# Four more channel units hand their four products to TensorE without an addition on VectorE, in a kernel ordered by hand-kept tables

## The chip, the cores and the metric

One core of one Trainium2 chip runs the kernel. The metric is the device time of one execution in microseconds, as a median over executions. A second number is the span of the profiled execution, from its first to its last recorded instruction.

## The reference

Two layers work on the same 2048 rows of 512 channels, and a gate mixes them. Cut to what is computed:

```python
g = sigmoid((x * gate_w).sum(-1, keepdims=True))
# a: a state-space convolution, 512 channels, 128 states each
dt = exp(log_dt)[:, None]; A = A_re + 1j*A_im; B = B_re + 1j*B_im; C = C_re + 1j*C_im
K = einsum("dn,dnl,dn->dl", C, exp((dt*A)[:,:,None] * arange(L)), dt*B).real   # kernel, L = 2048
y = irfft(rfft(pad(x.T)) * rfft(pad(K)))[:, :L].T                              # y in bf16
a = y + x * Dskip
# b: linear attention, 32 heads of 16, feature maps of two softmaxes
q, k, v = split(x @ wqkv)
phi(t) = concat(softmax(t @ w_phi), softmax(-(t @ w_phi)))
num = phi(q) @ (phi(k).T @ v);  den = phi(q) @ phi(k).sum(rows) + 1e-6
b = (num / den) @ wo
out = g * a + (1 - g) * b          # (1, 2048, 512), bf16
```

## The kernel before

**Front.** Parameters, `u` and the weights are loaded; twiddle tables (`TB`, `TI`, `TJ`) are made with sines on ScalarE; `wps` folds the feature map into the key and query weights (`WW`, `Wqp`); `xps` transposes `u` into `xT`. Polar forms of the state parameters become the tables `Ctab` and `Dtab`. The spectrum of `u` is made in two stages of matmuls, `psA` read out as `XAu` and `psB` read out as `xst`, and written to memory (`XUd`). The keys go in eight blocks of 256 rows: `pk` on TensorE, two exponentials `Ek` on ScalarE, a sum per head and sign `Zk` on VectorE, its inverse on ScalarE, `vp` read out as `vb`, the product `vr` on VectorE and `kn` (tile `kvp`) on TensorE. In some blocks TensorE first adds groups of four (`zk`, L718), which leaves VectorE a shorter reduction (L734 in place of two of L731).

**Convolution kernel.** The 512 channels are cut into 16 units of 32 (unit U holds channels 32U to 32U+31). For a unit the power of a state at position l is split in a coarse and a fine factor, both complex. ScalarE makes the fine factor's sines and cosines (`cs`) and its magnitude (`E`), VectorE extends `E` (`El`, L1049) and multiplies both into `R` (`Rh` L1119, `Rl` L1123). The coarse factor `A` is made from `Ctab` and `Dtab` by two products, L1102 and L1107. They are the real and the imaginary part of a sum, which a third instruction, L1112 (`A3`), forms in a unit whose digit in `FOURS` is 0; TensorE then contracts two parts of `A` with two of `R` in 64 matmuls. Where the digit is 1 there is no addition and TensorE takes all four products, 128 matmuls that add up in PSUM (L170, tile `kps`). `A` has one buffer, `R` two.

**Transforms.** `kps` is read out as `KD`, transformed (`psA` read out as `XA`, `psB` as `XK`), multiplied with the stored spectrum (`XUX`, product `t`, L1233, or L1236 for the last two units), transformed back (`psz`, read out as `Zr`; then through memory, `Zd` and `ZT`, or by a transpose on VectorE for the last 128 channels) and finished in `psy`, where the attention's output is added for the first three blocks of 128 channels; VectorE multiplies by the gate (L1370, L1373). The units of one 128-channel block share a transform; the last block's units 14 and 15 go singly.

**What sets the order.** Every step is a node of one plan (`Plan.add`, L102); nothing is scheduled by a compiler. `run` (L148) gives each engine its instructions in the order of the table `ORDER`, two letters a node. `SIDES` has one digit for each step that may run on either of two engines, mostly the read-outs out of PSUM: ScalarE or VectorE (`evict`, L562; helpers L144 on ScalarE, L146 on VectorE). `RINGS` says from which PSUM pool such a step takes its buffer. `WARM` gives the number of dummy matmuls that TensorE issues into a new PSUM tile ahead of its work (L1563); a digit counts only where the node takes a new tile. `ZPS` marks the key blocks with the pre-sum on TensorE. An engine works strictly in its own order, so an instruction that waits holds all behind it.

Buffers (L1440): `A`, `KD`, `XA`, `ax` one each; `R`, `E`, `XK`, `Zr` two; `XUX` three; `cs` four.

Of the kernel before, what the change touches and what calls it, by code (L numbers as in the profile page):

```python
# [70 lines left out]
class Plan:  # L71

    DIGITS = "0123456789abcdefghijklmnopqrstuvwxyzABCDEFGHIJKLMNOPQRSTUVWXYZ-_"
    ORDER = ("0B0C0D0H0I0J2P000K0L0M112R2t2v0S0U0_100V120W0P0y0z0A2y2u0N0T14150O0Q0Y0X0Z18172Q2S2w2x0405060s0t0u0d0e0f0708090g0h0i0102030j"
             "0k0l0a0b0c0m0n0o0p0q0r0v0w0x130R2T2V2U2W2X2Z2Y2J2K192-0-1a1c1u2H1w1l162I1F2_311x1m1y1n1d1G1H3330322z2A341v2B2F2D1b2C352E1e1A"
             "1C2G1z361D2N2L2O37392M1o1p1q0E0F0G1r1s1t1B1E1W3a1J384A4H4J4I4K4W4Y4X4Z4O4L3b3d4S4M4P3e4N4T4Q4U1N3c513f554R4V3h4-3g563i4_5052"
             "5357595a5b5c5d3j5g1O3k543l585k5l5o5p5h3m5e5f1K5i4B5q4C5m5r5s3P5t3n5v5z3p5j5n3o5w5A1I1Q5u5D5E5F5G5H3u1L3q5x5B3w3x5K5O5y5C5S5L"
             "4D3v5P1R3r3s3t3y3z3A5T5I3Q3R5J5M5Q5U5Z1S5V1X1T1U1P3B3D3E615N5W625X5Y3C5R5-4E635_653I673K1M66683J3L3S6064696k6m3T3V6l6n6o6c6a"
             "6p3W3U6b6q6d3X3Z3Y6r3_3-1V1Z1Y406e1-1_25216s206t6v41433M3N3O3F3G3H1f1g1h426g45444647492627484a4b4c4d4e4g284f4h6h2b6i292a2d2c"
             "224i4j4k4l4n4o2e2m2f232g242h6w2i2j2n4m2o6f6j2q2p2r2k4s4t4p4q4r1i1j1k2l2s4u4v4w4x4y4z6E6G8j6x8x8y6u8i8n8k8m8o8l6y8p8q4F8u6z4G"  # L80
             "8z6D8v8w8A8B6F6H6I8D8E8R6K7b8C8F8J8K8G8H8I6J6L6M8S7c6N7d7f7haf6O8X8T7e7g6P6Q8Yag7i8L7K8-7M6R6S6T6U9c9d9e6V6W6X6Z6-6_8M8_7j8N"
             "7O8P7L8O7k8Q7N8U8V94907l957m7n8W8Z7Pao7Qap7oa5a9aa919293ah6Y707p7q7r6A6B6C9f9g9h9i9j9k7s7t7u7w7x7y9697a6a87173abadalamaq74ai"
             "aj72akauav98759a99a79bacae7RanaC777SaD9o7T789p76aras7vaE7U7VataI7Wawax9waL7A7C9x9q9y7XaM7D9r9z9s9AaJc6c77zaFaG9EbY7E7G7FaN7Y"
             "7Z7-7_80818384858r8s8t9B9C9D9t9u9v9l9m9nb0b1b2c09Fc17BaRaHc882869GaSb-c39M9NayaA87azaBaKb_7H88898b7Ic4aOaPaQ9Occcd8abZ8c7J8d"
# [6 lines left out]
    SIDES = ("01110001001011111100111001000001010101110000001110000000000011101000101111111100010100010000000000000000000000000000"  # L91
             "0000000000000000000000000010000000000000000001100001001")
# [4 lines left out]
    FOURS = ("0111110101011000")  # L97
    ZPS = ("00000101")
# [1532 lines left out]
```

## Time and profile before

| | |
|---|---|
| median of 3 runs | 252.7 us (251.59 to 253.8) |
| profiled execution, its own time | 252.06 us |
| its span | 250.3 us |
| VectorE (DVE) busy | 234.2 us, 94% |
| ScalarE (ACT) busy | 221.2 us, 88% |
| TensorE (PE) busy | 206.6 us, 83% |
| mean granted TensorE clock | 0.957 |
| transfers | 34.86 MB, 139 GB/s |

"L178" is line 178 of the kernel, and a row names the tile written, an arrow, and the tiles read. In the rows of groups stand the count, the busy time, the mean of one in ns, and the idle time just before with its releaser; in the rows of the timeline the start, the length, and in brackets the wait before. In the rows of waits stand who waited for whom, the total, how often and the longest. L144 and L146 are helpers, so read-outs are told apart by their tiles.

### The profile page before, as it was taken

The page shows a single profiled execution, that of the slowest core. Times are in us where ns is not written, and L with a number is a line of the kernel's source. Part 1 is how long each engine was busy: PE and PEld are TensorE (multiplying, and loading weights), DVE is VectorE, ACT ScalarE, POOL GpSimd, SP SyncE. Part 2 cuts the span into 40 slices and gives each one's busy share as a digit, 9 for nine tenths or more (in the row PEclk, how much of TensorE's full clock was granted, in tenths as well). Part 3 has the DMA queues.
Part 4 walks back from the last instruction along what each step waited for, and adds up shares of the span by engine and source line. Part 5 has one row for each costly group of instructions (what it writes and reads, how often), then busy time and mean ns, then how long its engine had stood idle before and what let it go on. Part 6 is the DMA issues. An engine that isn't in the chain of part 4 may idle for free. (4 is left out here: it accounts for less than half of the span.)

```text
span 250.3 us, 9879 instructions
## 1 busy us (share of the span) xinstructions
PE 206.6 (83%) x4393; PEld 141.3 (56%) x4415; DVE 234.2 (94%) x318; ACT 221.2 (88%) x305; POOL 8.7 (3%) x21
## 2 busy tenths in 40 slices
PE   0675999999984685999988887999989789889960
PEld 0675656555754432365656645775678467777530
DVE  7999998899999999999999999999999999998880
ACT  3998998999999999999999999999999997892830
POOL 5700000000000000000000000000000000000000
PEclk9999999999997596899999999999999999999996
DMA  7997000080551755003787049723595989872934
GB/s 187 220 218 182 18 3 4 3 243 14 145 151 59 198 150 146 3 3 115 182 245 185 5 122 204 245 86 66 157 245 133 237 230 319 197 226 50 220 75 84
DMA packets 52842, 34.86 MB, mean 139 GB/s; under 512 B 30528, under 2 KB 48320, under 8 KB 52800
## 3 DMA queue, kind: packets, MB, share of 16 engines
q1 hardware_dynamic: 51744, 33.98, 53.4%
q8 instruction: 34, 0.56, 0.9%
q10 hardware_dynamic: 1056, 0.26, 0.5%
q14 instruction: 8, 0.07, 0.1%
HBM read 21.38 MB, written 12.58 MB: 136 GB/s over the span
## 5 line engine op out<-in xcount | busy, mean ns | idle before, releaser
L178 PE MATMUL kps<-R,A 128*32 128x64 bf16 x1600 | 29.1, 229 | 2.5 <-ACT XK L144 0.8
L178 PEld LDWEIGHTS <-A 128*32 128x32 bf16 x1600 | 27.2, 160 | 6.5 <-issue 3.0
L68 ACT ACTIVATE cs<-args 128x1024 bf16<-128x1024 f32 x32 | 30.6, 1050 | 0.0
L1102 DVE TENSOR_TENSOR A<-Ctab,Dtab 128x2048 bf16<-128x2048 bf16 x16 | 19.5, 1218 | 0.6 <-PE kps L178 0.6
L1123 DVE TENSOR_TENSOR R<-E,cs 128x2048 bf16<-128x2048 bf16 x16 | 19.5, 1218 | 0.0
L1107 DVE TENSOR_TENSOR A<-Ctab,Dtab 128x2048 bf16<-128x2048 bf16 x16 | 19.5, 1218 | 0.0
L1119 DVE TENSOR_TENSOR R<-E,cs 128x2048 bf16<-128x2048 bf16 x16 | 19.5, 1217 | 0.0
L144 ACT CAST XA<-psA 128x1024 bf16<-128x1024 f32 (+1 forms) x17 | 16.1, 986 | 2.5 <-PE psA L185 2.4
L144 ACT CAST Zr<-psz 128x1024 bf16<-128x1024 f32 (+1 forms) x16 | 15.8, 1025 | 2.0 <-DMA Zd<-Zr 1.6
L68 ACT ACTIVATE Ek<-pk 128x512 bf16<-128x512 f32 x32 | 16.6, 611 | 1.0 <-PE pk L704 1.0
L68 ACT ACTIVATE E<-args 128x1024 bf16<-128x1024 f32 x16 | 16.8, 1052 | 0.4 <-issue 0.2
L68 ACT ACTIVATE Eq<-pq 128x512 bf16<-128x512 f32 (+1 forms) x28 | 16.8, 688 | 0.3 <-PE pq L838 0.3
L1233 DVE TENSOR_TENSOR t<-XUX,XK 128x2048 bf16<-128x2048 bf16 x14 | 16.9, 1219 | 0.1
L144 ACT CAST XK<-psB 128x1024 bf16<-128x1024 f32 (+1 forms) x17 | 16.1, 981 | 0.6 <-DVE t L1233 0.6
L838 PE MATMUL pq<-xT,Wqp 128*128 128x512 bf16 x64 | 16.5, 395 | 0.1
L752 PE MATMUL vp<-WW,xT 128*128 128x512 bf16 x62 | 15.7, 380 | 0.1
L704 PE MATMUL pk<-WW,xT 128*128 128x512 bf16 x57 | 14.8, 380 | 0.5 <-issue 0.2
L611 PE MATMUL psB<-XAu,TB 64*128 64x128 bf16 x256 | 11.0, 241 | 3.8 <-ACT xst L144 2.6
L731 DVE TENSOR_REDUCE Zk<-Ek 128x64 f32<-128x1024 bf16 x12 | 14.0, 1210 | 0.0
L65 ACT ACT_TABLE_LOAD x10 | 12.8, 1283 | 0.9 <-PEq L1615 0.7
L611 PEld LDWEIGHTS <-TB 64*128 64x128 bf16 x256 | 9.0, 106 | 8.0 <-issue 7.9
L761 DVE TENSOR_TENSOR vr<-vb,vr 128x1024 bf16<-128x1024 bf16 x16 | 10.5, 683 | 1.7 <-ACT vr L68 1.5
(213 smaller groups left out, 506.4 us busy)
## 6 DMA issues: line engine op xcount, KB each, us to landing
XUX<-XUd SPq DMA_DIRECT2D x32, 256.0 KB, 4.9
XUd<-xst SPq DMA_DIRECT2D x8, 512.0 KB, 3.0
ax<-apd SPq DMA_DIRECT2D x16, 256.0 KB, 5.1
Zd<-Zr SPq DMA_DIRECT2D x24, 128.0 KB, 3.5
ZT<-Zd SPq DMA_DIRECT2D x6, 512.0 KB, 6.1
UD<-in_A_u_dram SPq DMA_DIRECT2D x16, 128.0 KB, 4.2
XUd<-xst SPq DMA_DIRECT2D x8, 256.0 KB, 4.0
wqk<-in_B_wqkv_dram SPq DMA_DIRECT2D x1, 1024.0 KB, 5.5
```

Source lines behind the costliest of these rows:

```text
L68: return self.nc.scalar.activation(**kw)
L144: self.nc.scalar.copy(out=o, in_=i)
L178: nc.tensor.matmul(kps[32 * dj:32 * dj + 32, g4, e, :], lhsT=A[:, ka, :, :, d].rearrange("p a b -> p (a b)"), rhs=R[:, kr, d, :], start=(i ...
L611: nc.tensor.matmul(box.ps[:, c2, sl, :], lhsT=fc.TB[rows, b0:b0 + 2].rearrange("p a b -> p (a b)"), rhs=X.t[rows, k, r0 + sl].rearrange("p ...
L704: nc.tensor.matmul(box.ps[:], lhsT=xT[:, st, kt, :], rhs=g.WW[:, kt, :], start=(kt == 0), stop=(kt == 3))
L752: nc.tensor.matmul(box.ps[:], lhsT=xT[:, st, kt, :], rhs=g.WW[:, 4 + kt, :], start=(kt == 0), stop=(kt == 3))
L838: nc.tensor.matmul(box.ps[:, m - m0, :] if late else box.ps[:], lhsT=g.Wqp[:, kt, 128 * m:128 * m + 128], rhs=xT[:, 4 * b:4 * b + 4, kt, : ...
L1102: nc.vector.tensor_tensor(out=c.A[:, 0:2].rearrange("p o a b c -> p (o a) b c"), in0=g.C[U // 8][:, 0:2, :, d0 % 256:d0 % 256 + 32].rearra ...
L1107: nc.vector.tensor_tensor(out=c.A[:, 2:4].rearrange("p o a b c -> p (o a) b c"), in0=g.C[U // 8][:, 1:3, :, d0 % 256:d0 % 256 + 32].rearra ...
L1119: nc.vector.tensor_tensor(out=c.R[:, :, :, 32:64], in0=t.E[:, 1].unsqueeze(1).to_broadcast([128, 2, 32, 32]), in1=t.cs[:], op=ALU.mult)
L1123: nc.vector.tensor_tensor(out=c.R[:, :, :, 0:32], in0=t.E[:, 0].unsqueeze(1).to_broadcast([128, 2, 32, 32]), in1=t.cs[:, ::-1, :, ::-1], o ...
L1233: nc.vector.tensor_tensor(out=box.t, in0=Ls[r0 // ns].X[:], in1=box.XK[:].unsqueeze(1).to_broadcast([128, 2, 1024]), op=ALU.mult)
```

## The change

`FOURS` has four more ones: units 0, 6, 8 and 10 lose the addition L1112 and get 128 matmuls in place of 64. Only units 13, 14 and 15 keep it. `ZPS` loses a one: a single key block (the eighth) keeps the pre-sum on TensorE, and the sixth goes back to two long reductions on VectorE. `ORDER`, `SIDES`, `RINGS` and `WARM` are new tables. The digits of `WARM` add up to 57 before and 76 now; in the built programs stand 45 dummy matmuls before and 61 now.

```diff
-    FOURS = ("0111110101011000")
-    ZPS = ("00000101")
+    FOURS = ("1111111111111000")
+    ZPS = ("00000001")
...
-    WARM = ("00000000000000610000000000002000060000000000000040000010000030000000000500050203000040000041500000000000100020000000"
+    WARM = ("00000000302140230000000500010000000000500005000002000021010153506010000100200200010000000300300200000000000000000000"
...
-    ORDER = ("0B0C0D0H0I0J2P000K0L0M112R2t2v0S0U0_100V120W0P0y0z0A2y2u0N0T14150O0Q0Y0X0Z18172Q2S2w2x0405060s0t0u0d0e0f0708090g0h0i0102030j"
+    ORDER = ("0B0C0D0H0K0L0I0J2P0M0_000S0U0P0N0O0V102t2u110W0405060y0z0A0s0t0u0a0b0c0g0h0i0102030d0e0f0j0k0l0708090m0n0o0p0q0r0v0w0x17120Q"
```

Read-outs change their engine in both directions. VectorE has now nine `XAu` in place of five, five `xT` out of `xps` in place of two, a `KD` of 1024 columns, two `XK` of 1024 and one of 512 and two `xT` of 512, which it had none of; it has four `vb` fewer, and one `xst`, one `WW`, two `wT`, two small `KD` and one small `xT` fewer. ScalarE has the others.

On VectorE, where the keys begin, just ahead of the first reduction of `Ek` to `Zk` (`psA` to `XAu` is the spectrum's first stage). Before:

```order
L377 TENSOR_TENSOR pt_226<-pmag,ppx 128x512
L412 TENSOR_SCALAR pb_228<-pt_227 128x256 x4
L146 CAST XAu<-psA 128x256x4
L731 TENSOR_REDUCE Zk<-Ek 128x64 x2
L146 CAST vb<-vp 128x512 x2
L761 TENSOR_TENSOR vr<-vb,vr 128x2x512 x2
L731 TENSOR_REDUCE Zk<-Ek 128x64 x2
```

The same place on VectorE now:

```order
L377 TENSOR_TENSOR pt_219<-pmag,ppy 128x512
L146 CAST XAu<-psA 128x256x4 x2
L377 TENSOR_TENSOR pt_219<-pmag,ppx 128x512
L731 TENSOR_REDUCE Zk<-Ek 128x64 x2
L146 CAST vb<-vp 128x512
L761 TENSOR_TENSOR vr<-vb,vr 128x2x512 x2
L731 TENSOR_REDUCE Zk<-Ek 128x64 x2
L146 CAST XAu<-psA 128x256x4 x2
```

Four read-outs of `XAu` stand here in place of one, one of `vb` has gone to ScalarE, and the four `pb` steps come later.

On VectorE at unit 6, in the middle of the program (`oT` is read out of the attention's `ops`). Before:

```order
L1102 TENSOR_TENSOR A<-Ctab_75,Dtab 128x2048
L1107 TENSOR_TENSOR A<-Ctab_75,Dtab 128x2048
L146 CAST oT_1977<-ops 128x512
L1049 TENSOR_TENSOR E<-E,Gtab 128x1024
L146 CAST oT_1976<-ops 128x512
L1119 TENSOR_TENSOR R<-E,cs 128x64x32
L1112 TENSOR_TENSOR A<-A 128x2048
```

Unit 6 on VectorE now:

```order
L1102 TENSOR_TENSOR A<-Ctab_75,Dtab 128x2048
L1123 TENSOR_TENSOR R<-E,cs 128x64x32
L909 TENSOR_TENSOR Eq<-Eq,ax 128x2048
L146 CAST oT_2011<-ops 128x512
L146 CAST XK<-psB 128x1024
L1107 TENSOR_TENSOR A<-Ctab_75,Dtab 128x2048
L146 CAST oT_2012<-ops 128x512
L1119 TENSOR_TENSOR R<-E,cs 128x64x32
L146 CAST oT_2011<-ops 128x512
```

The addition L1112 is gone, and a read-out of `XK` with 1024 columns, ScalarE's before, stands between the two products.

On VectorE in the last stage, from the third block's last output product (L1370) on; `t` out of `XUX` and `XK` is the product of the last 128 channels. Before:

```order
L1370 TENSOR_TENSOR xT<-psy,gT 128x4x128
L1233 TENSOR_TENSOR t<-XUX,XK 128x2048 x2
L146 CAST KD<-kps 128x256 x2
L1236 TENSOR_TENSOR t<-XUX,XK 128x2x512
L1373 TENSOR_TENSOR xT<-psy,gT 128x2x4x128
L146 CAST xT<-bps 128x2x128
L1236 TENSOR_TENSOR t<-XUX,XK 128x2x512
```

The last stage on VectorE now:

```order
L1370 TENSOR_TENSOR xT<-psy,gT 128x4x128
L1233 TENSOR_TENSOR t<-XUX,XK 128x2048
L1373 TENSOR_TENSOR xT<-psy,gT 128x2x4x128
L146 CAST XK<-psB 128x1024
L1233 TENSOR_TENSOR t<-XUX,XK 128x2048
L1236 TENSOR_TENSOR t<-XUX,XK 128x2x512 x2
L146 CAST XK<-psB 128x512
L1236 TENSOR_TENSOR t<-XUX,XK 128x2x512 x2
```

The two `t` of 2048 no longer stand together: an output product and a new read-out of `XK` come between them. Two small `KD` and an `xT` have left for ScalarE, and a second `XK` stands ahead of the last two short products.

42 lines of the change are left out of this document (21 added, 21 removed).

## The prediction

> **What bounds the kernel now.** I read the page first, then the busy time by stage, then what VectorE waited for.
>
> ```profile
> span 250.3 us, 9879 instructions
> PE 206.6 (83%) x4393; PEld 141.3 (56%) x4415; DVE 234.2 (94%) x318; ACT 221.2 (88%) x305; POOL 8.7 (3%) x21
> ```
>
> VectorE (DVE) is the fullest engine: 234.2 of 250.3 us. The stages below are cut at VectorE's own landmarks: the first key reduction (29.39), the end of the spectrum's last read-outs `XAu` (72.23), the first `El` (102.50), the third channel block's first products `t` (200.59), its last output product (226.89), the last instruction (243.21). Columns: stretch, length, then the busy time of PE, PEld, DVE, ACT, POOL, then the granted clock, the DMA share and GB/s.
>
> ```profile
> 0.00:29.39 29.39, 17.35 (x174) 14.65 (x176) 27.84 (x66) 24.21 (x33) 8.70 (x21) 1.00 0.84 176
> 29.39:72.23 42.84, 42.14 (x745) 25.81 (x750) 39.71 (x51) 40.59 (x77) 0.00 (x0) 1.00 0.28 82
> 72.23:102.50 30.27, 20.67 (x313) 11.18 (x316) 29.73 (x56) 29.64 (x33) 0.00 (x0) 0.72 0.40 115
> 102.50:200.59 98.09, 88.49 (x2203) 61.89 (x2208) 97.17 (x108) 96.46 (x129) 0.00 (x0) 1.00 0.55 143
> 200.59:226.89 26.30, 23.23 (x603) 18.75 (x599) 24.85 (x25) 21.03 (x23) 0.00 (x0) 1.00 0.83 229
> 226.89:243.21 16.32, 14.77 (x381) 9.03 (x379) 14.85 (x20) 9.27 (x15) 0.00 (x0) 1.00 0.58 131
> 243.21:250.30 7.09, 0.00 (x0) 0.00 (x0) 0.00 (x0) 0.00 (x0) 0.00 (x0) 0.68 0.43 76
> ```
>
> The second stage is TensorE's (42.14 of 42.84); there VectorE idles 3.13 us. From 72 to 200 us VectorE idles 0.54 and 0.92 us, so there a microsecond put on it or taken off it moves the end by one. The last two working stages hold 1.45 and 1.47 us of its idle time. These are its waits:
>
> ```profile
> DVE vr L761 <- ACT vr L68: 1.5, 3, 0.7
> DVE xT L1370 <- PE psy L1360: 1.3, 1, 1.3
> DVE t L1236 <- DMA XUX<-XUd: 1.0, 1, 1.0
> DVE Zk L734 <- PE zk L725: 0.6, 2, 0.4
> DVE A L1102 <- PE kps L178: 0.6, 1, 0.6
> ```
>
> So the question is what the change does to VectorE's own sum, and whether these waits grow or shrink.
>
> **The change part by part.** VectorE's prices:
>
> ```profile
> L1112 DVE TENSOR_TENSOR A<-A 128x2048 bf16<-128x2048 bf16 x7 | 8.5, 1218 | 0.0
> L731 DVE TENSOR_REDUCE Zk<-Ek 128x64 f32<-128x1024 bf16 x12 | 14.0, 1210 | 0.0
> L146 DVE CAST vb<-vp 128x512 bf16<-128x512 f32 x11 | 7.5, 685 | 0.4 <-PE vp L752 0.3
> L146 DVE CAST XAu<-psA 128x1024 bf16<-128x1024 f32 x5 | 5.9, 1217 | 0.3 <-PE psA L586 0.3
> L146 DVE COPY wT<-wtp 128x1024 bf16<-128x1024 bf16 x4 | 2.6, 678 | 0.0
> L734 DVE TENSOR_REDUCE Zk<-zk 128x128 f32<-128x512 f32 x2 | 1.4, 692 | 0.6 <-PE zk L725 0.6
> L146 DVE COPY xT<-xps 128x1024 bf16<-128x1024 bf16 x2 | 1.4, 681 | 0.0
> ```
>
> ```profile
> 114.71 1.22 DVE L1102 TENSOR_TENSOR A<-Ctab,Dtab 128x2048 bf16<-128x2048 bf16 x1
> 115.85 1.22 DVE L1107 TENSOR_TENSOR A<-Ctab,Dtab 128x2048 bf16<-128x2048 bf16 x1
> ```
>
> The two products of the second fence start 1.14 us apart, 0.08 less than one lasts: instructions overlap by that much. So what VectorE pays per instruction is the mean less 0.08: 1.14 for a 1218 ns one, 0.60 for one of 680 to 690 ns.
>
> *First three stages, to 102.5 us.* Gone: unit 0's addition (1.14), four `vb` (2.42), one `xst` (1.14, as `XAu`), one `WW` (1.13, same form as `XAu`), two `wT` (1.20), one `zk` reduction (0.61): 7.6 us. Added: four `XAu` (4.55), three `xT` (1.80), two full key reductions because one block's pre-sum on TensorE is switched off (2.26): 8.6 us. Sum +1.0. (The gate's two 128x16 instructions go from this stage to the next; I leave them out of both.) On ScalarE up to the first `E`:
>
> ```profile
> L144 ACT CAST XAu<-psA 128x1024 bf16<-128x1024 f32 x11 | 10.8, 1023 | 0.2 <-PE psA L586 0.2
> L144 ACT CAST vb<-vp 128x512 bf16<-128x512 f32 x5 | 2.9, 601 | 0.4 <-PE vp L752 0.4
> L144 ACT COPY xT<-xps 128x1024 bf16<-128x1024 bf16 x6 | 6.0, 1013 | 1.0 <-PE xps L499 1.0
> ```
>
> ```profile
> 33.61 1.93 ACT L144 CAST XAu<-psA 128x1024 bf16<-128x1024 f32 x2
> ```
>
> Two in a row last 1.93 us, so the second adds 0.91, and ScalarE's overlap is some 0.12; one costs 0.90, a `vb` 0.48: four `XAu` go (-3.6), three `xT` (-2.7), and come four `vb` (+1.9), an `xst` and a `WW` (+1.8), two `wT` (+1.8), and a pair of `Eq` now ahead of the first `E` (+0.95): +0.15. TensorE loses eight `zk` matmuls, one 1.1 us piece:
>
> ```profile
> 58.41 1.09 PE L725 MATMUL zk<-Ek,ident 128*128 128x256 bf16 x8
> ```
>
> and it is the full engine of the second stage, where VectorE's +1.0 can hide in 3.13 us of idle time. Bounds: +1.0 if nothing hides, -1.5 if half of that idle time goes. I take -0.4, half of TensorE's 1.1 less one dummy, since ScalarE's +0.15 at the next hand-over stops more.
>
> *Fourth stage, to 200.6 us.* Gone: three additions (units 6, 8, 10), -3.42. Added: an `XK` (1.14) and a `KD` (1.14; neither form stands on VectorE before, the nearest is `XAu`, also 1024 columns out of PSUM, and no row is dearer), and two `xT` of 512 columns (1.20, as `vb`): +3.48. An `Eq` product leaves the stage and an `R` enters it. Sum +0.1. **The saving of the change is spent here on read-outs that ScalarE did.** ScalarE gets about 2.8 us lighter, but it was not the last to arrive. I keep the 0.58 wait:
>
> ```profile
> 171.27 1.23 DVE L1102 TENSOR_TENSOR A<-Ctab,Dtab 128x2048 bf16<-128x2048 bf16 x1 [0.58 <-PE kps L178]
> ```
>
> *TensorE's side.* A unit's kernel product costs, with two and with four products:
>
> ```profile
> 105.51 1.21 PE L178 MATMUL kps<-R,A 128*32 128x64 bf16 x64 [0.51 <-DVE R L1123]
> ...
> 110.55 2.25 PE L178 MATMUL kps<-R,A 128*32 128x64 bf16 x128
> ```
>
> So +1.04 for each of four units, 4.2 us, and 16 ns for one more matmul. The built programs hold 45 dummies before and 61 now (the table's 76 counts some that are never issued), 16 more. It hides under VectorE's 98 us, where TensorE has 9.6 us free. [...]
>
> *Fifth stage.* The same work in another order. It is set by the chain from the last `t` through the transfers of `Zr` and `ZT` to `psy`, whose end VectorE awaited for 1.25 us. Order and rings along it are alike; I take 0, from -1.4 (its idle time gone) to +0.5.
>
> *Last stage.*
>
> ```profile
> 226.89 0.69 DVE L1370 TENSOR_TENSOR xT<-psy,gT 128x512 bf16<-128x512 f32 x1 [1.25 <-PE psy L1360]
> 227.50 2.35 DVE L1233 TENSOR_TENSOR t<-XUX,XK 128x2048 bf16<-128x2048 bf16 x2
> ...
> 233.62 0.69 DVE L1236 TENSOR_TENSOR t<-XUX,XK 128x1024 bf16<-128x1024 bf16 x1 [1.05 <-DMA XUX<-XUd]
> ```
>
> ```profile
> 228.74 1.62 SPq L1188 DMA_DIRECT2D XUX<-XUd  x2
> ```
>
> The last `XUX` load goes out when the first `t` frees its buffer (228.6) and is there at 233.62, 5.0 us later. Now an output product, a 1024 `XK` and the other `t` (1.14 each) and one `t32` (0.60) stand between: 4.0 us, so a wait of 1.0 remains and hides the large `XK` as it hid `KD` and `xT` before. The 512 `XK` (0.60) comes after it, uncovered. I take +0.5, from 0 to +0.9 (a later `Zr` for the three transposes that now stand together). Two of the late stores go to ScalarE's queue behind its last read-out, as two others did: nothing.
>
> **Sum:** -0.4 + 0.1 + 0 + 0.5 = +0.2 us. The profiled execution took 252.06 us (span 250.3 and 1.76 around it), so 252.3. That lies just under the median of the runs shown, 252.7, and among them (251.59 to 253.8), so I make no further correction. The terms' bounds, which won't all fall to one side, make 250.8 to 254.0 for this case alone.
>
> **The rivals.**
>
> *The waits go (faster).* The order is new everywhere, so it may pack better. If the front takes its lower bound (-1.5), the 0.58 wait goes against +0.1, and the 1.25 us before the output product goes too while the tail costs +0.5: -1.5 - 0.5 - 1.25 + 0.5 = -2.75, 249.3 us. For it: TensorE, full in the second stage, loses a 1.1 us `zk` there, and half of the 0.6 us that VectorE waited for `zk` goes with it. Against it: the 1.25 us end with transfers, and no shorter path for them shows in the order.
>
> *TensorE is late at kernel products (slower).* `A` has one buffer, so unit u+1's first product waits until unit u's matmuls have read it, and now units 0 to 12 all read it for 2.25 us, where four of them took 1.21. The place: after unit 8's 128 matmuls TensorE has 16 `psB`, 16 `pq` and four `args` before unit 9's.
>
> ```profile
> 171.92 1.89 PE L838 MATMUL pq<-xT,Wqp 128*128 128x512 bf16 x8
> 181.47 1.06 PE L191 MATMUL psB<-XA,TB 128*128 128x128 bf16 x16
> 179.93 0.39 PE L1041 MATMUL args<-selE,statE 64*128 64x512 bf16 x2
> ```
>
> That is 2.25 + 1.06 + 3.7 + 0.7 + 2.25 = 10.0 us from the end of unit 8's second product to the end of unit 9's matmuls. VectorE meanwhile does two `E`, the next `R` and `A` pairs (5.8), another `R` pair and two `t` (4.5): 10.3. Then comes the `KD` read-out, new on VectorE, and it waits for just these matmuls; unit 10's products and all that follows on VectorE are queued behind it. So 0.3 us of lateness decides. If each of units 8 to 12 brings the 0.58 us of the row at 171.27, that is +2.9, and 252.06 + 0.2 + 2.9 = 255.2. Against it: one such wait in all of before.
>
> [...]
>
> *It does less than it says:* VectorE loses four additions and still gains 1.0 + 0.1 in the first four stages and, in the last, the two `XK` (1.74) less two small `KD` and an `xT` that go to ScalarE (about 0.33 each, an estimate from their 128x256 form at a quarter of `XAu`): 1.8 us of work in all. That is in the forecast.
>
> **How the numbers follow.** Likeliest (252.3): 0.58. Waits go (249.3): 0.23. TensorE late (255.2): 0.19. About 1% (2.5 us) is what a measurement here can tell from no change, so against 252.7 faster means below 250.2 and slower above 255.2. Faster: 0.18 of the second case and 0.02 of the first, 0.20. Slower: 0.12 of the third (it may come only in part) and 0.02 of the first, 0.14. The same: 0.66. For 8 in 10 the range runs from 249.3 to 255.4, to about the middle of either rival.
>
> **What would show it.** VectorE's busy sum near 236 us, against 234.2, whatever the span; if it falls, my count is wrong. ScalarE near 217. Unit rows of 128 kernel matmuls at 2.25 us thirteen times. A first `El` near 102.1. The waits on `psy` and `XUX` near 1 us each. Waits of `A` or `KD` on `kps` over 1.5 us in all mean the slower rival; a second stage with under 2 us of VectorE's idle time and no `psy` wait mean the faster one. The prediction is wrong if VectorE's idle time before its last instruction, 9.0 us in before (243.21 less 234.2), moves by more than 2 us.

## The result, and the profile after

Both kernels were timed side by side, 18 executions each. The changed kernel takes 254.39 us (253.34 to 256.46), the kernel before 253.37 us (251.41 to 254.57). The ratio is 1.0066, with a 95% interval of 1.0044 to 1.0087. So it lies within the 1% that was called no change, but it is slower by more than its interval, where the sum had said 0.2 us over the profiled execution. The profiled execution of the changed kernel took 254.0 us, 1.9 more than that of before (252.06). Ratios, here and below, leave out executions that took over 1.5% longer than the fastest of the same kernel: none of these 36, but three of the six of after_phase, for example.

The head of its page, then the stages cut at the same VectorE landmarks (columns as before: stretch, length, busy time of PE, PEld, DVE, ACT, POOL, granted clock, DMA share, GB/s):

```profile
span 252.2 us, 10424 instructions
PE 213.5 (85%) x4679; PEld 144.8 (57%) x4679; DVE 235.7 (93%) x317; ACT 217.9 (86%) x303; POOL 8.2 (3%) x21
```

```profile
0.00:29.79 29.79, 19.25 (x178) 15.73 (x179) 28.34 (x63) 24.77 (x34) 8.21 (x21) 1.00 0.83 173
29.79:71.67 41.88, 40.73 (x739) 25.00 (x738) 40.20 (x52) 40.62 (x76) 0.00 (x0) 1.00 0.33 90
71.67:101.41 29.74, 22.26 (x341) 11.05 (x341) 29.40 (x54) 29.71 (x36) 0.00 (x0) 1.00 0.47 134
101.41:202.35 100.94, 92.70 (x2445) 65.14 (x2446) 97.70 (x110) 92.05 (x121) 0.00 (x0) 0.98 0.48 130
202.35:229.87 27.52, 23.83 (x602) 18.61 (x596) 24.85 (x24) 21.16 (x23) 0.00 (x0) 1.00 0.76 222
229.87:245.67 15.80, 14.77 (x398) 9.31 (x392) 15.15 (x20) 9.63 (x17) 0.00 (x0) 1.00 0.55 129
```

VectorE's sum is 235.7 us, where 236 was forecast, and ScalarE's 217.9, where 217 was. The lengths tell where the 1.9 us of the span came from:

| stage | before | after | change | forecast |
|---|---|---|---|---|
| first three, to the first `El` | 102.50 | 101.41 | -1.09 | -0.4 |
| fourth, to the third block's `t` | 98.09 | 100.94 | +2.85 | +0.1 |
| fifth, to the last output product | 26.30 | 27.52 | +1.22 | 0 |
| last | 16.32 | 15.80 | -0.52 | +0.5 |
| behind VectorE's last instruction | 7.09 | 6.53 | -0.56 | 0 |

In the fourth stage VectorE is busy 0.53 us longer (97.17 before) and idle 2.32 us longer (3.24 against 0.92). In the fifth its work is the same 24.85 us, so all of the 1.22 is waiting. The rows of these waits on VectorE's timeline, the wait in brackets:

```profile
133.80 1.23 DVE L909 TENSOR_TENSOR Eq<-Eq,ax 128x2048 bf16<-128x2048 bf16 x1 [1.38 <-DMA ax<-apd]
177.73 2.36 DVE L1233 TENSOR_TENSOR t<-XUX,XK 128x2048 bf16<-128x2048 bf16 x2 [0.73 <-DMA XUX<-XUd]
218.39 0.69 DVE L1370 TENSOR_TENSOR xT<-psy,gT 128x512 bf16<-128x512 f32 x1 [1.21 <-PE psy L1360]
220.52 0.69 DVE L1049 TENSOR_TENSOR E<-E,Gtab 128x1024 bf16<-128x1024 bf16 x1 [1.43 <-ACT E L68]
```

Only the third has a like in the fourth and fifth stage of before, and that one stood at another place there. What the first two wait for stands on SP's queue (start, length of the issuing, tiles, how many):

```profile
121.89 3.59 SPq L1186 DMA_DIRECT2D XUX<-XUd  x6
126.70 2.81 SPq L902 DMA_DIRECT2D ax<-apd  x4
...
151.51 21.06 SPq L1276 DMA_DIRECT2D Zd<-Zr  x8
172.67 2.45 SPq L1186 DMA_DIRECT2D XUX<-XUd  x4
```

`ax` has one buffer. It is free at 126.67, when the two products of the first batch row end; the loads go out at 126.70, behind 1.5 MB of `XUX`, and VectorE wants the result from 132.42 on; it is there at 133.80. In before the same product started at 137.52. The second place is SP's own order: eight `Zd` stores, of which the last four wait for their `Zr`, hold the four `XUX` loads back until 172.67, and the first `t` needs one 5 us later. In before those loads went out from 154.34 on. The fifth stage's wait on `E` is ScalarE's order:

```profile
214.99 1.01 ACT L144 CAST Zr<-psz 128x1024 bf16<-128x1024 f32 x1 [1.61 <-DMA Zd<-Zr]
217.13 1.01 ACT L144 CAST Zr<-psz 128x1024 bf16<-128x1024 f32 x1 [1.14 <-DMA Zd<-Zr]
218.17 1.28 ACT L65 ACT_TABLE_LOAD   x1
219.46 1.94 ACT L68 ACTIVATE E<-args 128x1024 bf16<-128x1024 f32 x2
```

Two `Zr` that wait for stores stand ahead of the table load and of both `E`. In before the table load stood ahead of the first `Zr`, and an `E` between the two.

### The profile page after: what moved, and what is told of

Same layout as the page of the kernel before. It is cut to its first block, busy times and chain, and to the rows that moved or that the text cites. A ratio compares the mean times of both kernels' runs of the same rounds, so it can differ in the third digit from the quotient of the medians.

```text
span 252.2 us, 10424 instructions
## 1 busy us (share of the span) xinstructions
PE 213.5 (85%) x4679; PEld 144.8 (57%) x4679; DVE 235.7 (93%) x317; ACT 217.9 (86%) x303; POOL 8.2 (3%) x21
## 3 DMA queue, kind: packets, MB, share of 16 engines
q1 hardware_dynamic: 51456, 33.78, 51.3%
## 4 chain that ended last, share of the span: by engine, by line
PE 34%; DVE 25%; ACT 19%; DMA 8%; issue 8%; SPq 4%; POOL 0%; DVEq 0%; ACTq 0%; POOLq 0%
PE pk L704 5%; PE kps L178 5%; PE vp L752 4%; DMA ax<-apd 4%; ACT cs L68 3%; PE pq L838 3%; ACT trg L68 2%; ACT Zr L144 2%; DMA Zd<-Zr 2%; PE psA L586 2%; SPq L1276 2%; DVE A L1102 2%; DVE A L1107 2%; DVE t L1233 2%; DVE R L1119 2%
## 5 line engine op out<-in xcount | busy, mean ns | idle before, releaser
L178 PE MATMUL kps<-R,A 128*32 128x64 bf16 x1856 | 33.7, 229 | 2.2 <-issue 1.3
L178 PEld LDWEIGHTS <-A 128*32 128x32 bf16 x1856 | 31.5, 161 | 5.7 <-issue 3.6
L731 DVE TENSOR_REDUCE Zk<-Ek 128x64 f32<-128x1024 bf16 x14 | 16.4, 1209 | 0.0
L752 PE MATMUL vp<-WW,xT 128*128 128x512 bf16 x64 | 16.3, 380 | 0.0
L704 PE MATMUL pk<-WW,xT 128*128 128x512 bf16 x64 | 15.5, 380 | 0.0
L144 ACT CAST XK<-psB 128x1024 bf16<-128x1024 f32 (+1 forms) x14 | 13.8, 1011 | 0.7 <-PE psB L191 0.7
L1262 PE MATMUL psz<-t,TI 128*128 128x512 bf16 x48 | 12.0, 380 | 0.7 <-DVE t L1233 0.3
L1049 DVE TENSOR_TENSOR E<-E,Gtab 128x1024 bf16<-128x1024 bf16 x16 | 10.9, 682 | 1.4 <-ACT E L68 1.4
L144 ACT CAST xst<-psB 128x1024 bf16<-128x1024 f32 x12 | 12.0, 1038 | 0.1
```

The lines of the kernel that those rows point to most:

```text
L144: self.nc.scalar.copy(out=o, in_=i)
L178: nc.tensor.matmul(kps[32 * dj:32 * dj + 32, g4, e, :], lhsT=A[:, ka, :, :, d].rearrange("p a b -> p (a b)"), rhs=R[:, kr, d, :], start=(i ...
L704: nc.tensor.matmul(box.ps[:], lhsT=xT[:, st, kt, :], rhs=g.WW[:, kt, :], start=(kt == 0), stop=(kt == 3))
L731: nc.vector.tensor_reduce(out=K.Z[:, u].rearrange("p g h -> p (g h)"), in_=K.E[:, u].rearrange("p g (h f) -> p (g h) f", f=16), axis=mybir ...
L752: nc.tensor.matmul(box.ps[:], lhsT=xT[:, st, kt, :], rhs=g.WW[:, 4 + kt, :], start=(kt == 0), stop=(kt == 3))
```

## The experiments

All ratios are to the kernel before, timed on the same chip in the same session. The kernels compute the same as the two kernels, unless a line says otherwise. Four theories, by the letters of the texts on record: **A**, VectorE's sum sets the end and the new waits on transfers ate the gain; **B/T**, TensorE's longer kernel products cost; **F**, the saving was handed back on the read-outs; and **K**, formed after unit0_four, that it is TensorE's instructions. Other letters are explained where they stand.

| run | edit | ratio | 95% interval |
|---|---|---|---|
| the change | | 1.0066 | 1.0044 to 1.0087 |
| em_later | after, one `Eq` product later | 0.9984 | 0.9946 to 1.0023 |
| act_order | after, ScalarE's `E` ahead | 1.0057 | 1.0019 to 1.0096 |
| ax_first | after, `XUX` behind `ax` | 1.0062 | 1.0028 to 1.0096 |
| em_and_act | em_later and act_order | 0.9944 | 0.9906 to 0.9982 |
| xux_early | em_and_act, `XUX` ahead of `Zd` | 0.9979 | 0.9952 to 1.0007 |
| both_light | em_and_act, one `XUX` behind `ax` | 0.9967 | 0.9925 to 1.0010 |
| fours_only | before, four units changed | 1.0231 | 1.0184 to 1.0279 |
| order_only | after, four additions back | 1.0291 | 1.0245 to 1.0337 |
| readouts_back | after, four read-outs back | 1.0241 | 1.0199 to 1.0283 |
| fours_readouts | fours_only, read-outs as in after | 1.0280 | 1.0246 to 1.0314 |
| no_dummies | after without dummies | 1.0110 | 1.0071 to 1.0149 |
| thirteenth_unit | em_and_act, unit 13 too | 1.0090 | 1.0058 to 1.0121 |
| unit0_four | before, unit 0 changed | 1.0283 | 1.0234 to 1.0332 |
| pe_time | before, TensorE's 1 us alone | 0.9997 | 0.9962 to 1.0031 |
| pe_count | before, 128 instructions alone | 1.0227 | 1.0153 to 1.0302 |
| unit0_phase | unit0_four, 128 more instructions | 1.0035 | 0.9993 to 1.0077 |
| after_phase | after, 128 more instructions | 1.0106 | 1.0028 to 1.0184 |
| count_light | pe_count, one `XUX` pair later | 1.0260 | 1.0201 to 1.0319 |

### The waits on transfers

**em_later.** VectorE's order around the first wait:

```diff
 L146 CAST wo<-ops
-L909 TENSOR_TENSOR Eq<-Eq,ax
 L146 CAST wo<-ops
 L1119 TENSOR_TENSOR R<-E,cs
 L1123 TENSOR_TENSOR R<-E,cs
+L909 TENSOR_TENSOR Eq<-Eq,ax
 L1102 TENSOR_TENSOR A<-Ctab,Dtab
```

> Changed kernel with the first product of Eq and ax for the second batch row moved on VectorE behind the next three instructions (a wo read-out and a pair R), 2.8 us of other work. Theory A (waits on transfers that the new order made): the 1.38 us wait on ax goes and the end comes 1.0 to 1.4 us earlier, 1.001 to 1.003 of before. Rival C (the time is set by transfers further on, XUX and Zd, which are issued by their own queue): the 1.38 us comes back as a longer wait on XUX (0.73 now) and at the last third, and the ratio stays 1.005 to 1.008.

Ratio 0.9984, against 1.0066: theory A's value or better. The row of the product has no wait left:

```profile
134.94 1.22 DVE L909 TENSOR_TENSOR Eq<-Eq,ax 128x2048 bf16<-128x2048 bf16 x1
```

By the two intervals (half widths 0.0038 and 0.0021, taken together 0.0044) the move is worth 0.8%, give or take 0.4: 1 to 3 us. One instruction three places too early cost about what its row said, 1.38 us, or more.

**act_order.** On ScalarE, with `E`'s matmul on TensorE moved ahead to match:

```diff
+L65 ACT_TABLE_LOAD
 L144 CAST Zr<-psz
+L68 ACTIVATE E<-args
 L144 CAST Zr<-psz
-L65 ACT_TABLE_LOAD
-L68 ACTIVATE E<-args x2
+L68 ACTIVATE E<-args
```

> Changed kernel with ScalarE's order of before in front of the last El: table load ahead of the two Zr, the first E between them, and its args ahead of the second psz on TensorE. Theory A: VectorE's 1.43 us wait on E goes and the end comes 1.0 to 1.4 us earlier, 1.001 to 1.003 of before. Rival C (the two Zr wait for Zd transfers, and psy waits behind the same): the 1.43 us moves to the following waits on psy and XUX, 1.005 to 1.008 of before.

The ratio, 1.0057, is rival C's. The trace is not as simple:

```profile
135.35 1.22 DVE L909 TENSOR_TENSOR Eq<-Eq,ax 128x2048 bf16<-128x2048 bf16 x1 [3.35 <-DMA ax<-apd]
220.25 0.68 DVE L1049 TENSOR_TENSOR E<-E,Gtab 128x1024 bf16<-128x1024 bf16 x1
```

```profile
101.46:204.21 102.75, 91.88 (x2443) 64.89 (x2446) 97.54 (x111) 92.29 (x121) 0.00 (x0) 0.98 0.48 128
204.21:229.93 25.72, 24.09 (x602) 18.71 (x599) 24.86 (x25) 21.05 (x23) 0.00 (x0) 1.00 0.80 238
```

The wait on `E` is gone and the fifth stage takes 25.72 us in place of 27.52. But 85 us earlier, where nothing was edited, the wait on the `ax` loads is 3.35 us, where it was 1.38 in the profiled execution of after, 2.0 us longer. The length of that wait was not the same in these two executions, so one trace can't say what the second move gains in the mean.

**em_and_act**, both moves:

> Changed kernel with both moves: the product of Eq and ax three instructions later, and ScalarE's order of before in front of the last El. Theory A (both waits cost what VectorE's rows say, and the second one's gain was hidden in its own run by an ax wait 2.0 us longer): 1.4 + 1.4 us less than the changed kernel, 0.990 to 0.996 of before. Rival C (the Zd transfers set the last third, E's place does not matter): no better than the first move alone, 0.997 to 1.001.

0.9944, in the range of theory A and 1.2% below the changed kernel (half width 0.4%). Against em_later alone the step is 0.4%, with a half width of 0.5%: not resolved.

**ax_first.** SP issues the six `XUX` loads after the four `ax` loads; every other engine's order stays.

```diff
-L1186 DMA XUX<-XUd x6
 L902 DMA ax<-apd x4
-L1186 DMA XUX<-XUd x4
+L1186 DMA XUX<-XUd x10
```

> Changed kernel with one change on SP's queue: the six XUX loads of 256 KB issued from 121.9 us on go behind the four ax loads. Theory A, in the form that the ax wait is a matter of the traffic ahead of it: ax lands in under 5 us from its issue instead of 7.1, the wait of 1.38 us at 133.8 goes, 1.000 to 1.003 of before. Rival D (the ax loads take 7 us whatever stands ahead, as 7.8 us in the kernel before): the wait stays over 1 us, 1.005 to 1.008, or more where the XUX loads then come late for t.

The mechanism of the wait is as theory A had it: `ax` landed in 4.0 us (median of the four; 6.3 in after), and the product started at 131.84 without a wait. But the time stayed:

```profile
138.80 0.60 PE L928 MATMUL ops<-Eq,KVbd 128*128 128x256 bf16 x4 [2.23 <-DVE A L1107]
```

```profile
131.84 1.21 DVE L909 TENSOR_TENSOR Eq<-Eq,ax 128x2048 bf16<-128x2048 bf16 x1
140.92 1.22 DVE L1233 TENSOR_TENSOR t<-XUX,XK 128x2048 bf16<-128x2048 bf16 x1 [1.59 <-ACT XK L144]
```

TensorE now stood for 2.23 us in front of four `ops` matmuls (the `A` that its row names had ended 0.6 us before), so `psB` and `XK` came late, and VectorE lost 1.59 us there in place of 1.38. The loads had moved into a moment in which something else was on its way, by the last group of runs TensorE's own instructions.

**xux_early** and **both_light** build on both moves. The first lets four `XUX` loads out ahead of four `Zd` stores, on SP:

```diff
-L1276 DMA Zd<-Zr x8
+L1276 DMA Zd<-Zr x4
 L1186 DMA XUX<-XUd x4
+L1276 DMA Zd<-Zr x4
```

> The kernel with both moves (em later, ScalarE's order) and on SP's queue the two XUX loads that t waits for at 177.7 us issued ahead of four Zd stores instead of behind them. Theory A: t's remaining wait there (0.15 to 0.8 us over the runs so far) goes: 0.1 to 0.7 us less, 0.991 to 0.995 of before. Rival C (the next wait on the XK or kps behind it takes it over): 0.994 to 0.997, as without it.

The wait of `t` at 177 went, as theory A said, and the ratio is 0.9979, above the ranges of both theories: no gain over 0.9944, and by the intervals no loss either. With both_light (below, 0.9967) the three kernels that hold both moves lie at 0.994 to 0.998, about 0.4% under the kernel before and 1% under the changed one. That is the best that was run. The single differences among them are not resolved.

### One part without the other

**fours_only** and **order_only** are the two halves:

```diff
-    FOURS = ("0111110101011000")
+    FOURS = ("1111111111111000")
```

in the kernel before, and the reverse in the changed one.

> Kernel before with one table changed: units 0, 6, 8 and 10 also hand over four products; order, read-outs, rings and dummies of before. Theory A (VectorE's sum sets the end, and the new kernel lost its gain in what was made anew around the four units): four additions of 1.14 us go, 4.6 us, of which 3.0 to 4.6 reach the end: 0.982 to 0.988 of before. Theory B (TensorE's longer kernel products, 4 x 1.04 us, come back as waits of the first product or of the read-outs): 0.995 to 1.005, with VectorE's idle time up by 3 us or more.

> Changed kernel with the additions of units 0, 6, 8 and 10 put back, all else as changed. Theory A: four instructions of 1.14 us come back on VectorE; the waits on ax (1.38) and on E (1.43) can take up a little, so 3.0 to 4.6 us more than the changed kernel: 1.018 to 1.025 of before. Theory B: the kernel products get 4.2 us shorter on TensorE and what it cost comes back, so 1.005 to 1.012 of before.

Both are far slower than either kernel. With the old order the four saved additions turn a kernel of 253 us into one of 258; in the new order the same four additions cost 5.7 us (1.0291 against 1.0066), more than their 4.6 us of work. Theory B's bound for the first was too low, theory A's sign wrong. VectorE's waits in fours_only (who waits for whom, total, how often, longest):

```profile
DVE A L1102 <- PE kps L178: 7.4, 6, 3.8
```

That is the forecast's slower rival, nearly to the letter: `A`'s one buffer, TensorE late. It did not come with the change, since the change came with an order made for it (0.4 us of such waits in after). order_only is no clean measure of the additions, because they stand where the new order had let them fall: TensorE waits 6.4 us for two of them. And both runs add or take 512 of TensorE's instructions, which the last group shows to matter: fours_only's trace has 2.9 us of the gaps described there, so not all of its loss is the price of the longer products.

**readouts_back** changes no instruction of TensorE: an `XK`, a `KD` and two `xT` of the fourth stage go back to ScalarE.

```diff
-L146 CAST XK<-psB 128x1024
-L146 CAST KD<-kps 128x1024
-L146 CAST xT<-bps 128x512 x2
+L144 CAST XK<-psB 128x1024
+L144 CAST KD<-kps 128x1024
+L144 CAST xT<-bps 128x512 x2
```

> Changed kernel with four read-outs of the fourth stage given back to ScalarE, in the same place of the order: an XK and a KD of 1024 columns and two xT of 512. Theory F (the saving was handed back on these): VectorE loses 1.14 + 1.14 + 0.60 + 0.60 = 3.5 us, and 2.0 to 3.5 of it reach the end, 0.993 to 0.999 of before. Theory A (ScalarE, 92 us busy of the stage's 101, cannot take 3 us more without coming late to what VectorE needs next): 1.003 to 1.012, with new waits of VectorE on ScalarE or on t's XK.

Theory F, which is how the prediction put it ("the saving of the change is spent here on read-outs that ScalarE did"), falls: VectorE is 2.8 us lighter and the kernel 1.75% slower than the changed one, at twice the loss that theory A allowed. First VectorE's waits, then TensorE's rows and ScalarE's around the longest of them, 3.38 us in front of the `A` at 171.52:

```profile
DVE A L1102 <- PE kps L178: 6.1, 5, 3.4
DVE Eq L909 <- DMA ax<-apd: 3.2, 3, 2.2
```

```profile
166.17 0.22 PE L821 MATMUL bps<-diagD,xT 128*128 128x128 bf16 x1
168.90 0.39 PE L1041 MATMUL args<-selE,statE 64*128 64x512 bf16 x2 [2.52 <-ACT cs L68]
169.22 2.26 PE L178 MATMUL kps<-R,A 128*32 128x64 bf16 x128
```

```profile
166.42 0.58 ACT L144 CAST xT<-bps 128x512 bf16<-128x512 f32 x1 [2.02 <-PE bps L821]
166.90 1.95 ACT L68 ACTIVATE cs<-args 128x1024 bf16<-128x1024 f32 x2
```

An `xT` that went back stands ahead of two `cs` on ScalarE and waits there for its `bps`; the `cs` come late, TensorE waits 2.5 us for them, and its 128 matmuls hold `A`. So the read-outs that VectorE took are not where the saving was lost; in this order they are what lets TensorE feed the four products in time.

**fours_readouts** tried whether they are enough in the old order. It is fours_only with this on top (and one `oT` each way):

```diff
-L144 CAST XK<-psB 128x1024
-L144 CAST KD<-kps 128x1024
-L144 CAST xT<-bps 128x512 x2
+L146 CAST XK<-psB 128x1024
+L146 CAST KD<-kps 128x1024
+L146 CAST xT<-bps 128x512 x2
```

> Kernel before with the four units changed and the fourth stage's read-outs split between the engines as in the changed kernel (an XK, a KD and two xT to VectorE, one oT each way), order, rings and dummies of before. Theory H (ScalarE's read-outs are what makes TensorE and so the first products late; moving them is the other half of the change): the waits of A on kps fall from 7.4 us to under 3, VectorE's work is that of before, and the time is 1.000 to 1.010. Rival (the order is needed, whoever reads out): the waits stay over 5 us and the moved read-outs add to them, 1.020 to 1.040.

Half of theory H holds: the waits of `A` fall from 7.4 to 3.0 us. But 3.0 us for an `xT` and 2.2 for `XUX` come in their place, and the ratio is 1.0280. So the read-outs alone don't bring the gain in the old order. That the order is the other half is likely but not shown by this run, since its 512 instructions more shift TensorE's code, and its trace has 4.7 us of the gaps of the last group.

**no_dummies** has only zeros in `WARM`, so 61 dummies less:

> Changed kernel without dummy matmuls (all 61). Theory E (the dummies cost: TensorE has 213.5 us of work, and they stand in front of kernel products): up to 2 us less than the changed kernel, 0.999 to 1.005 of before. Theory A (they hide under VectorE): 1.004 to 1.008 if the granted clock stays over 0.95, and more where it falls to 0.7 in a stage, as it was in the third stage of before, and TensorE gets late there.

1.0110, against theory E: without the dummies the kernel is some 0.4% slower than with them (half width 0.45%, so hardly resolved). The clock granted in the third stage falls from 1.00 to 0.80 without them:

```profile
71.80:101.50 29.70, 20.14 (x312) 10.32 (x312) 29.36 (x54) 29.14 (x34) 0.00 (x0) 0.80 0.46 134
```

TensorE is busy for 20.14 us of this stage, where it is 22.26 in after; in before 20.67 went with 0.72. But the first stage of after, with 19.25 us of 29.79, was granted 1.00, so these rows show that the clock was lower without the dummies and not what sets it. This run also has 122 of TensorE's instructions less, and TensorE stands for 1.4 us in front of a `psy` matmul (L1360) in the way that the next part describes; what the clock and what the instructions cost is not told apart.

**thirteenth_unit**, on top of both moves:

```diff
-    FOURS = ("1111111111111000")
+    FOURS = ("1111111111111100")
```

> The kernel with both moves, and the next unit (13) hands over four products as well: one addition (1.14 us at 209 us) less on VectorE, 64 matmuls (1.04 us) more on TensorE. Theory A (VectorE's sum): 0.6 to 1.1 us less, 0.990 to 0.993 of before. Rival C (the fifth stage is set by the chain through psz, Zd and psy, on whose transfers VectorE waits 1.4 us anyway, and the longer kernel product stands in that chain on TensorE): 0.994 to 1.000.

1.0090, 1.5% above its base and above rival C's range too. The waits of `A` on `kps` are 2.5 us and those on `psy` 3.8. One more of the same edit turns the best kernel into one slower than before. How much of it is the longer product stays open, since the 128 instructions more also shift TensorE's code: behind 228 us its trace has three of the gaps that the next part describes, 3.5 us together, where em_and_act's has none over 0.25.

### TensorE's instructions

**unit0_four** has one digit changed in the kernel before:

```diff
-    FOURS = ("0111110101011000")
+    FOURS = ("1111110101011000")
```

> Kernel before with one digit changed: unit 0 alone hands over four products. Its addition stands in the first stages, before the kernel products of the fourth. Theory G (an addition pays where TensorE has time: only the units whose products TensorE cannot follow cost): 0.5 to 1.1 us less than before, 0.995 to 0.998. Rival: it is the new form itself that costs, 1.003 or more.

1.0283, in the rival's range and far up in it: an addition less on VectorE and 64 matmuls more at the start of the fourth stage cost 7 us. Its trace has TensorE standing in the middle of groups, waiting for nothing that the profile shows:

```profile
135.99 0.27 PE L858 MATMUL zs<-Eq,SZw 128*32 128x256 bf16 x1
137.62 0.29 PE L858 MATMUL zs<-Eq,SZw 128*32 128x256 bf16 x3 [1.36 <-issue]
...
138.95 1.58 PE L178 MATMUL kps<-R,A 128*32 128x64 bf16 x85
141.62 0.89 PE L178 MATMUL kps<-R,A 128*32 128x64 bf16 x43 [1.10 <-issue]
```

From the first gap to the second stand 35 `zs`, 8 `psB` and 85 `kps` matmuls, 128 in all, with their weight loads 256 instructions. Three more gaps stand near the end, the last of them in TensorE's last group:

```profile
228.78 0.22 PE L821 MATMUL psy<-diagD,xT 128*128 128x128 bf16 x1 [0.85 <-issue]
232.50 0.37 PE L178 MATMUL kps<-R,A 128*32 128x64 bf16 x10 [0.72 <-issue]
247.80 0.47 PE L1360 MATMUL psy<-ZT,TJ 64*32 64x32 bf16 x42 [1.86 <-issue]
```

The page of before lists transfers of instructions:

```profile
q8 instruction: 34, 0.56, 0.9%
```

34 transfers of 0.56 MB are 16.5 KB each. If the 8830 matmuls and weight loads that its program has for TensorE fill them, one takes 64 bytes by this estimate, and 256 fill one transfer, as many as stand from the first gap to the second. The count of transfers goes with TensorE's instructions: 34 at 8830, 35 at 9086 (unit0_phase), 36 at 9358 (the changed kernel) and 37 at 9486 (after_phase), each time as often as 256 goes into them. That the gaps lie at the ends of such pieces is the author's reading, here and below; no row marks where a piece ends.

Four kernels separate TensorE's time from its instructions. **pe_time** adds the microsecond (seven wide dummies, 14 instructions), **pe_count** the 128 instructions in a place where TensorE is idle:

```diff
+L1563 MATMUL kps<-TB,ident 128x512 x7
 L178 MATMUL kps<-R,A 32x64 x64
```

> Kernel before with seven dummies of 512 columns (some 1.5 us, 14 instructions) in front of unit 0's kernel matmuls, where TensorE waits 0.5 us for R: its end comes about 1.0 us later, as with four products, and hardly an instruction is added. The additions stay. Theory T (it is TensorE's time there that costs): 1.010 to 1.03 of before. Theory K (it is the number of instructions, which the core must fetch in time): 0.998 to 1.004.

```diff
-L1563 MATMUL psB<-TB,ident 128x512 x6
+L1564 MATMUL psB<-TB,ident 128x32 x70
 L611 MATMUL psB<-XAu,TB 64x128 x16
```

> Kernel before with 70 dummies of 32 columns in place of the six of 512 columns in the third stage at 85.6 us, where TensorE stands idle for 1.8 us: 128 more instructions, as unit 0's four products add, and about the same time. Theory K (instruction transfers of 16 KB each, of which the later ones now fall behind the XUX and ax loads at 125 to 135 us, so that TensorE runs dry in the middle of a group): gaps of 1 us and more within zs or kps groups after 130 us, 1.010 to 1.03 of before. Theory T: 0.998 to 1.004.

0.9997 and 1.0227: it is the instructions. In pe_count the first two gaps stand at the same two instructions, and the three late ones (1.06, 0.44 and 1.55 us) do too:

```profile
137.42 0.29 PE L858 MATMUL zs<-Eq,SZw 128*32 128x256 bf16 x3 [0.94 <-issue]
...
140.87 0.88 PE L178 MATMUL kps<-R,A 128*32 128x64 bf16 x43 [0.57 <-issue]
```

**unit0_phase** is unit0_four with the edit of pe_count, 256 instructions in all, so that the pieces end again where they ended in before:

> Unit 0 with four products (1.028 of before) and the same 128 instructions added once more in the third stage as narrow dummies, 256 in all, so that the 16 KB pieces of TensorE's code end at the instructions where they ended before. Theory K with the piece's end as cause: the gaps at 136 and 141 us go, 0.995 to 1.005 of before. Theory K with only the number as cause, or theory T: 1.02 to 1.035, no better than without.

1.0035, as theory K with the piece's end had it, with 256 instructions more than before where 128 more cost 2.8%. So as far as these four show it, neither time nor number sets the price, but where the pieces of 256 end. The traces say the same. Behind 100 us the gaps over 0.2 us that end in "issue" add up to 5.9 us in unit0_four and 5.5 in pe_count, whose profiled executions are 5.8 and 5.2 us longer than that of before; to 0.5 in pe_time; and there is none in before and in unit0_phase. A sum of gaps is no price in itself, though: em_and_act, with the lowest ratio of all, has 2.9 us of them.

**after_phase** shifts the changed kernel by 128:

```diff
-L1563 MATMUL psB<-TB,ident 128x512 x2
+L1564 MATMUL psB<-TB,ident 128x32 x66
```

> Changed kernel with 66 dummies of 32 columns in place of two of 512 in the third stage: 128 more instructions, nearly the same time. Theory K: the gap of 1.3 us that TensorE shows in the middle of a kps group at 194.4 us (83 matmuls, then the gap, then 45) goes or moves elsewhere, and the time changes by over 0.5% of before either way (1.0066 now). Theory T: the gap stays where it is and the ratio is 1.004 to 1.009.

1.0106 (interval to 1.0184): slower, by less than its interval can separate from the change itself, so the time decides nothing. The gap at 194 us left its place, as theory K had it, and one of 2.25 us came at 126.6, in a profiled execution of 259.2 us. The changed kernel has 528 instructions more than before (9358 against 8830), two pieces and 16, so at its end its pieces lie nearly as they did.

Why is a piece late? **count_light** takes 0.5 MB of loads away from 125 us in pe_count. **both_light** does so on top of both moves at the gap of the changed kernel, which stands between 83 and 45 matmuls of one `kps` group (1.33 us in after, 1.97 in em_and_act). On SP's queue:

```diff
 L1513 DMA wo<-in_B_wo_dram
-L1186 DMA XUX<-XUd x4
+L1186 DMA XUX<-XUd x2
 L902 DMA ax<-apd x4
 L895 DMA apd<-apm x2
+L1186 DMA XUX<-XUd x2
```

> The kernel with 128 more instructions (1.023 of before), and on SP's queue the second pair of XUX loads of 125 us (0.5 MB of the 2.5 MB that are issued from 124.4 to 130.8) issued 18 us later, still ahead of the t that reads it. Theory K (the piece of TensorE's code comes late because it shares the DMA engines with these loads): it lands about 1.5 us earlier, the gap of 0.94 us at 137 goes, 1.000 to 1.012 of before. Rival (the gap is the latency of a fetch that TensorE's shifted code asks for too late, whatever the traffic): 1.018 to 1.028.

```diff
-L1186 DMA XUX<-XUd x2
 L1276 DMA Zd<-Zr x2
 L902 DMA ax<-apd x4
+L1186 DMA XUX<-XUd x2
```

> The kernel with both moves (em later, ScalarE's order; 0.994 of before), and on SP's queue one pair of XUX loads that went out at 190.6 us put behind the ax loads of 193 us. Theory K: TensorE's gap of 1.97 us in the kps group at 194 shrinks, and with it the waits of A (0.8) and of t for XK (0.9) behind it: 0.988 to 0.993 of before. Rival (the gap comes of 256 instructions in 2.25 us, faster than code arrives, whatever the traffic; or the later XUX makes t wait): 0.994 to 1.000.

In before a piece moves between 131 and 132 us. In pe_count none does between 128 and 134, while 0.48 to 0.74 MB of data move in each 2 us, and the next one follows between 134 and 135. In count_light that one moves between 133 and 134, some 1 us sooner, and both gaps fall under 0.1 us (ahead of the second TensorE now also waits 0.5 us for `E`). ax_first has a third such place: its 2.23 us stand eleven times 128 matmuls ahead of the gap of the changed kernel, and the next piece moved between 136 and 137 us there, among the `XUX` loads that had been put later, and between 133 and 134 in after. In both_light a piece moves between 190 and 192 us, where in em_and_act one moves between 192 and 194; the gap shrinks and the waits of `A` and `t` behind it vanish (em_and_act first, then both_light, then its fourth stage):

```profile
194.49 0.95 PE L178 MATMUL kps<-R,A 128*32 128x64 bf16 x45 [1.97 <-issue]
```

```profile
192.78 0.94 PE L178 MATMUL kps<-R,A 128*32 128x64 bf16 x45 [0.37 <-issue]
```

```profile
101.44:200.14 98.70, 91.11 (x2487) 65.33 (x2490) 97.44 (x111) 92.71 (x121) 0.00 (x0) 1.00 0.50 134
```

So lighter traffic brought the code sooner in count_light and both_light, and heavier traffic later in ax_first, each in one trace; the fourth stage of both_light is back at 98.70 us (98.09 before, 100.94 in after). But both times lie in the rival's range, 1.0260 and 0.9967. Count_light's profiled execution, of 263.3 us, still has 5.5 us of gaps, as many as pe_count's: those at 137 and 141 are gone, and one of 1.74 us that ends at 165.6 has come. The three places fit a delay of code by traffic; that it is all of the 2.3% of pe_count is not shown.

What sets the rest stays open, but the rows fit a second reading. From the end of the first gap to the end of the second TensorE goes through one piece; that takes 4.00 us in unit0_four, of which 1.10 are the gap, and 3.45 in pe_count, of which 0.57 are. A kernel product uses up 128 matmuls in 2.25 us. So a piece that TensorE runs through fast may end before the next one is there, whatever else moves, and where the pieces end decides how fast each is used up. No run tests this alone.

## Why the prediction was right or wrong

**Right.** VectorE's sum (235.7 for 236) and ScalarE's (217.9 for 217); the time inside the range and within 1%; the slower rival's condition, which in after came to 0.4 us of waits. By its own last test, VectorE's idle time before its last instruction, it moved from 9.0 to 10.0 us, less than the 2 named. But that test was too wide to catch the miss: the forecast's own terms, 1.8 us more work for 0.2 us more time, asked for an idle time some 1.6 us shorter, and it came out 1.0 us longer.

**The step that failed: the fourth stage, "+0.1", in which of 0.92 us of idle time only the 0.58 wait was carried over.** It was +2.85. Of this 0.53 is work, 0.34 of it the gate's two small instructions, which the prediction saw cross the landmark and left out. The other 2.32 is idle time, 1.38 and 0.73 of it on `ax` and `XUX`. The prediction saw that "an `Eq` product leaves the stage" and counted it as work that moves. It did not ask when the tile that the other products read is free and how long its load takes: the buffer is free at 126.67, the product can start 7.1 us after the load's issue, and its new place is 5.75 us behind. em_later shows that this one place cost about as much as the whole loss. For `XUX` the same question was asked only in the last stage, where the sum had it on SP's row.

**The front, -0.4,** was -1.09. VectorE's work grew by 0.66 us, as counted (+1.0 less the gate's 0.34), and its idle time fell by 1.75, 1.45 of it in the second stage; the forecast had 1.4 of idle time go. So the term held but for 0.35 us of idle time. Its lower bound was not worked out as it says: half of 3.13 us is 1.57, and against 1.0 of work that makes -0.6, not -1.5.

**The fifth stage, 0 with +0.5 as upper bound,** was +1.22. "Order and rings along it are alike" was read off the chain to `psy`; ScalarE's `E`, behind two waiting `Zr`, is not in that chain. act_order removes the wait and 1.8 us of the stage in its trace; in whole times its share is not resolved.

**The last stage, +0.5,** was -0.52. The wait of 1.05 us on `XUX` was to stay at 1.0 and went: its two loads landed 2.5 and 3.3 us after their issue, where they had taken 3.0 and 4.4 in before, so a landing time read off one trace did not hold. The 0.60 us of the small `XK` is there.

**TensorE's term,** 4.2 us hidden under VectorE, was priced by time alone. pe_time (0.9997) agrees that a microsecond there cost nothing. What has a price are the instructions: pe_count's 128 cost 2.3%, unit0_four's, with its longer product, 2.8%. That the changed kernel's own loss has a part from this (the gap of 1.33 us, with 0.2 us of VectorE's wait behind it in after) is likely small: em_later's trace has 1.86 us there and the kernel is faster, and both_light, which shrinks the gap, is no faster than em_and_act.

**The reading of the saving,** that it is spent on read-outs, is right as a count of work, since VectorE's sum rose by 1.5 us. As a reading of what could be won back it fell with readouts_back: the four read-outs are what the four products need in this order. What the changed kernel lost stands as waits, and two moves of one to three places, one in VectorE's order and one in ScalarE's (with the matmuls that feed it), take it back: 0.994 to 0.998 of before.

## What to carry to other kernels

When an order is made anew, follow each moved instruction that reads a transfer back to the moment when its buffer is free, add the landing time of a like transfer, and compare with its new place; work counted by engine can be right to 0.5 us and miss 2 us of such waits. A part of a change that looks like a price (here read-outs given to the fuller engine) may be the condition for the rest, so try the halves apart before blaming one. And count the instructions of an engine that issues thousands: 128 more moved the time by 2.3 to 2.8% here and 256 more by 0.35%, so that a change of a single digit has to be compared with a control that adds only the instructions.

## What the runs showed of the hardware

The page's queue q8 moved 34 transfers of instructions of 16.5 KB in before and 36 in the changed kernel, as TensorE's instructions went from 8830 to 9358; the page counts them as 0.9% and 1.0% of the time of the 16 transfer engines, the data on q1 as 53.4% and 51.3%. 128 instructions more cost 2.3 to 2.8% (pe_count, unit0_four), 256 more 0.35% (unit0_phase; the interval holds zero), and 1 us of TensorE's time without them nothing (0.9997, give or take 0.35%). The gaps show in the rows as "issue", mostly in the middle of one group of matmuls, and the first two of unit0_four stand 128 matmuls apart.

The wait on one and the same `ax` loads differs by 2 us between two executions (1.38 us in after, 3.35 in act_order, on the same edit-free stretch), so a wait on a transfer read off one trace can have an error as large as itself.
